# Two heads in one transfer, zero fills on the load queue, a guarded loop, and new weights for a list scheduler

## The chip, the cores and the metric

The kernel runs on one core of a Trainium2 chip. The metric is the device time of one execution in microseconds. TensorE (PE) does the matrix products, VectorE (DVE) and ScalarE (ACT) the elementwise work, GpSimd (POOL) some elementwise work and the indirect transfers, and SyncE (SP) only issues transfers between the chip's memory and the on-chip buffers.

## The reference

Three stages follow each other. Attention has 4 batches, 8 heads, 576 positions and head size 64, and each position sees itself and the 63 before it. Its output, 2304 tokens of 512 numbers, goes through a gated MLP (MoE1, width 2048), and the result through a routed layer (MoE2): a token whose skip score is positive goes to the best of 8 experts (width 1024), the others stay as they are.

```
# attention: scores = q k^T / 8 in a causal window of 64, softmax, times v
h = x @ w_in
sp = np.where(h > 20.0, h, np.log1p(np.exp(np.minimum(h, 20.0))))
x = (h * np.tanh(sp)) @ w_out
...
do_compute = x @ w_skip > 0
logits = x[do_compute] @ w_gate
e_idx = np.argmax(logits, axis=1)
gate_w = softmax(logits)[e_idx]
...
out[do_compute] = x + gate_w * (np.maximum(x @ w1[e], 0.0) @ w2[e])
```

## The kernel before

The 2304 tokens are cut into 6 blocks of 384. For each block there are 4 pairs of heads, 24 pairs in all. For a pair, SP loads q and k (`lqk`) and v (`lv`); S is the scores' matmul, then the softmax on DVE and ACT, PT the transposes of the probabilities, PV the product with v, and xH and xL the two parts of the block's input to MoE1 for that pair's 128 columns (a high part in a rounded format and the rest, so that two or three fast matmuls replace a slow exact one). MoE1 goes over 16 chunks of 128 hidden columns for each block, so 96 chunks: L1 (into `ph`), then mn on DVE, four passes on ACT (u), g on DVE, gH and gL, and L2 (into `po`). The first block's L2 takes the whole weights and is exact; all others take high and low parts. The parts of the weights (cv, ca, w) are also made on DVE and ACT. The first L2 needs all of a chain: PV of pair 3, xH and xL of pair 3, the first chunk's L1, mn, u, g.

The first 8 pairs (`load_nat`, L413) have q and k loaded in the natural layout, in tiles nq and nk that hold four rows and two heads per partition, and transposed on PE (`nat_T`). The others (`load_dvt`) are transposed on DVE. A block that crosses from one batch into the next has two runs of rows, so twice as many transfers. `keep_warm` (L1163) puts dummy matmuls named warm in PE's gaps before the first L2 and at the end of MoE1.

After its MoE1 each block is routed: xs is the evacuated output (`x_evac`, L828), lp or lg the logits, then a chain of small DVE operations (r_mx, r_z, r_oh ...) with a position matmul pp on PE, and the rows are scattered into the table xg_d, by expert. That table must be zero before the first scatter: `fill_zero` sets a tile named nothing to zero on DVE (task fz), `fill_slots` copies it into xg_d (task fs, 17 transfers, on POOL's queue). Every second fill has an fz of its own, and that one waits until the two fills before it have landed. The last block's three tiles go another way to the first experts: xsH and xsL are parts of xs, pick is a 0/1 matrix from the routing, and sel = pick x (xsH + xsL) on PE (24 matmuls for the three tiles) gives the first expert's input at once, which is copied to xgT; E1 is the experts' first matmul (L1221). After all experts, `overflow_round` runs as often as an expert has more tokens than its slots: here not once.

What order the work has is decided when the kernel is built, by a list scheduler (`Plan`, L44). Each task has an engine or a choice of engines with a cost, what it must come after, the buffers it takes, and a due time. The scheduler goes through time, gives each free engine the task that is most urgent, and writes the instructions in that order. Due times are made from T0, D0, D1 and others (first chunk's time and the chunks' distance), shifted by LATE for each kind of task; PRICE, LEAN and SLACK weigh the choice between engines. None of these numbers is known to the chip: each engine runs its instructions in the order written, and waits on semaphores. Transfers on SP take eight semaphores in turn, so that a transfer is issued only when the one eight before it has landed.

Of the kernel before, what the change touches and what calls it, by code (L numbers as in the profile page):

```python
# [22 lines left out]
N1 = 144  # L23


T0, D0, D1, US, UO, WO, LO = 32.22, 5.11, 4.4, 1.64, 5.74, 8, 1.94


LAST = []
GAP, FILL = 0.15, 0.8  # L30
E2B = 0.3
X0 = 2.6
FILL_AT, FILL_BY = 17, 6.0
PRICE3 = dict(P=0, V=0.0, A=0.12, G=0.2, S=0)
AHEAD = 18
EARLY = 8
# [122 lines left out]
TW0 = 38.08
PRICE0 = dict(P=0, V=1.12, A=0.09, G=-0.5, S=0)  # L160
TW = 90.61
PRICE2 = dict(P=0, V=0.99, A=0.94, G=0, S=0)
PRICE = dict(P=0, V=2.15, A=1.08, G=0.63, S=0)
LAT = {("V", "V"): 0.13, ("A", "A"): 0.13, ("A", "V"): 0.14, ("V", "A"): 0.13, ("P", "P"): 0.05}
LATE = dict(wl=-8.1, wa=0.23, wo=0.67, ws=-0.46, wH=-12, lqk=-1.57, nT=-0.3, S=-4.68, ex=4.29, nm=-2.8, PT=-1.37, Pe=4.82, xH=-9.25, L1=0.07, L2=-1.13, me=3.5, n=-5.7, mn=-0.18, ln=2.32, r=-1.08, g=3.72, gH=0.53, xe=7.4, rT=0.57, re=5.95, rl=1.1)
LEAN = {('kT', 'A'): 0.67, ('qT', 'A'): 0.05, ('nm', 'A'): 0.31, ('xH', 'A'): -1.38, ('wo', 'A'): 0.09, ('wH', 'A'): -0.16, ('n', 'A'): -1.26, ('re', 'A'): -0.13, ('xe', 'A'): -0.29, ('nm', 'G'): 1.25, ('wL', 'G'): -0.62, ('gL', 'G'): 1.5}
SLACK = dict(P=0.26, V=0, A=0, G=0.17, S=0.0)


@with_exitstack  # L170
def tile_kernel(
# [24 lines left out]
    XW = DM + 2  # L196
# [4 lines left out]
    xg_d = dram.tile([NE * CAP, XW], F32, name="xg_d")  # L201
# [17 lines left out]
    for p0 in (0, 64):  # L219
        sl = maskA[p0:p0 + 64]  # L220
# [123 lines left out]
    ex = [(e, j) for e in range(NE) for j in range(EW)]  # L344
# [49 lines left out]
    def load_v(pr, dma=SP):  # L394
        blk, hp = divmod(pr, 4)
        vt = rqp.tile([128, 6, 2, D], F32, tag="vt", name="vt", bufs=3)
        vts[pr] = vt
        for g, n, b, s0 in runs(blk):
            z = 2 if s0 == 0 else 0
            if z:  # L400
                G.memset(vt[0:64, 3 * g], 0.0)
            w0 = 3 * g
            if z:
                dma.dma_start(out=vt[64:128, w0], in_=v[b, 2 * hp:2 * hp + 2, 0:64].rearrange("j s d -> s j d"))
                w0 += 1
            lo = s0 + 64 * (w0 - 3 * g) - 64
            nw = 3 * (g + n) - w0
            for j in range(2):
                src = bass.AP(tensor=v.tensor, offset=v[b, 2 * hp + j].offset + D * lo,
                              ap=[[D, 128], [64 * D, nw], [1, D]])  # L410
                dma.dma_start(out=vt[:, w0:w0 + nw, j], in_=src)

    def load_nat(pr):  # L413
        blk, hp = divmod(pr, 4)
        nq = rqp.tile([128, 4, 2, D], F32, tag="rk", name="nq", bufs=4)
        nk = rqp.tile([128, 4, 2, D], F32, tag="rk", name="nk", bufs=4)
        r0 = 0
        for g, n, b, s0 in runs(blk):
            t0 = max(s0 - 64, 0)
            nr = (s0 + 192 * n - t0) // 4  # L420
            for j in range(2):
                SP.dma_start(out=nk[r0:r0 + nr, :, j],
                             in_=k[b, 2 * hp + j, t0:s0 + 192 * n].rearrange("(p r) d -> p r d", r=4))
            for j in range(2):
                SP.dma_start(out=nq[48 * g:48 * (g + n), :, j],
                             in_=q[b, 2 * hp + j, s0:s0 + 192 * n].rearrange("(p r) d -> p r d", r=4))
            r0 += nr
        nat[pr] = (nq, nk, r0)

# [152 lines left out]
    for pr in range(NU // 2):  # L582
        t = unit_time(2 * pr) - 5
        if pr < NPE:
            T(("lqk", pr), one(SS, 2.62 if len(runs(pr // 4)) == 1 else 5.2), lambda e, pr=pr: load_nat(pr), lat=2.3,
              get=[("rk", ("nq", pr)), ("rk", ("nk", pr))], due=t, t0=.7)
            for i in (1, 0):
                T(("nT", pr, i), one(PP, .36), lambda e, pr=pr, i=i: nat_T(pr, i), after=[("lqk", pr)] + ([("S", pr - 1)] if pr else []),
                  get=[(f"po{i}" if pr < 4 else "ps", ("tqk", pr, i))], use=[("nq", pr) if i == 0 else ("nk", pr)])
        else:  # L590
            T(("lqk", pr), one(SS, 3.6 if len(runs(pr // 4)) == 1 else 7.2), lambda e, pr=pr: load_dvt(pr), lat=2.3,
              get=[("rq", ("nq", pr)), ("rk", ("nk", pr))], due=t - 5)
        nd = sum(3 if r[3] == 0 else 2 for r in runs(pr // 4))
        T(("lv", pr), [("S", SP, .53 * nd)], lambda e, pr=pr: load_v(pr, e), lat=2.3,
          get=[("vt", ("vt", pr))], due=unit_time(2 * pr))
    for pr in range(NU // 2):
        if pr < NPE:
# [5 lines left out]
        else:  # L603
# [6 lines left out]
          after=pre + ([("PT", 2 * pr + j - DEEP) for j in range(2)] if early and 2 * pr >= DEEP else []) + ([] if early else [("PT", 2 * pr - 1)]),  # L610
# [89 lines left out]
    for f in range(NF):  # L700
        for kind in ("in", "out"):
# [269 lines left out]
    NS = NE * CAP // 128  # L971
# [6 lines left out]
    def fill_slots(n):  # L978

        if n < NS:  # L980
            G.dma_start(out=xg_d[128 * n:128 * n + 128, :DM].rearrange("p (a c) -> p a c", c=128),
                        in_=nothing[:, :, :128].to_broadcast([128, DM // 128, 128]))
        else:
            G.dma_start(out=xg_d.rearrange("(n p) c -> p n c", p=128)[:, :, DM:XW], in_=nothing[:, :, 128:].to_broadcast([128, NS, 2]))

    for n in range(NS + 1):
        tf = chunk_time(int(FILL_AT)) + FILL_BY * (n // 2)
        if n % 2 == 0:
            T(("fz", n), one(VV, .2), lambda e: fill_zero(), due=tf, t0=tf, after=[("fs", x) for x in range(max(n - 2, 0), n)])
# [442 lines left out]
```

## Time and profile before

| | us |
|---|---|
| time, median of 3 runs | 706.64 (705.81 to 707.05) |
| the profiled execution's time | 707.58 |
| its span in the trace | 705.8 |
| PE busy | 684.6 |
| DVE busy | 444.9 |
| ACT busy | 397.7 |
| POOL busy | 82.0 |

The span goes from the first to the last instruction in the trace; the time has the launch's own edges too. Busy means that the engine worked on data, so the time in which an engine only issues transfers or waits is not in it. [...]

### The profile page before, as it was taken

How to read it: one execution, taken by the hardware profiler on the slowest of the kernel's cores; microseconds unless marked ns; L12 is line 12 of the kernel's file. 1: busy time of each engine (PE TensorE's matmuls, PEld its weight loads, DVE VectorE, ACT ScalarE, POOL GpSimd, SP SyncE). 2: the span in 40 equal slices, each digit the busy share in tenths (PEclk: the TensorE clock that was granted, in tenths of full speed). 3: DMA queues.
4: the chain of work that ended last, by engine and by line, in shares of the span. 5: the costliest groups of instructions: out<-in, count | busy, mean ns of one | idle time of the engine just before them, and what ended most of it. 6: DMA issues, size and time to landing. Idle time of an engine off the chain costs nothing. (4 is left out here: it accounts for less than half of the span.)

```text
span 705.8 us, 13633 instructions
## 1 busy us (share of the span) xinstructions
PE 684.6 (97%) x4921; PEld 583.3 (83%) x4921; DVE 444.9 (63%) x1261; ACT 397.7 (56%) x975; POOL 82.0 (12%) x145
## 2 busy tenths in 40 slices
PE   7999999999999999999999999999999999999993
PEld 7786766788788888888888888888888898998982
DVE  5899999786656556665567655447576553565250
ACT  5778886676666666676556666555652432322220
POOL 3000000212220001000020001012243021111011
PEclk9999999999999999999999999999998999999997
DMA  7889996975523222231221100054472775778000
GB/s 176 210 216 245 283 245 150 207 185 127 110 59 84 41 37 62 46 90 38 39 48 48 51 1 11 19 189 139 133 223 100 253 267 199 270 281 314 1 25 20
DMA packets 141693, 92.54 MB, mean 131 GB/s; under 512 B 110205, under 2 KB 118429, under 8 KB 141616
## 3 DMA queue, kind: packets, MB, share of 16 engines
q1 hardware_dynamic: 137568, 82.90, 42.9%
q0 software_dynamic: 4048, 8.63, 4.1%
q8 instruction: 45, 0.74, 0.4%
q14 instruction: 32, 0.26, 0.1%
HBM read 73.96 MB, written 17.86 MB: 130 GB/s over the span
## 5 line engine op out<-in xcount | busy, mean ns | idle before, releaser
L738 PE MATMUL ph<-xH,w 128*128 128x384 f32 x768 | 222.6, 351 | 1.2 <-DVE g L765 0.5
L789 PE MATMUL po<-w,gH 128*128 128x512 f32 x480 | 152.8, 400 | 0.0
L738 PEld LDWEIGHTS ph<-xH,w 128*128 128x128 f32 x768 | 141.0, 188 | 11.2 <-issue 5.1
L738 PE MATMUL ph<-xL,w 128*128 128x384 f32 x384 | 130.0, 338 | 0.0
L789 PEld LDWEIGHTS po<-w,gH 128*128 128x128 f32 x480 | 88.0, 188 | 14.8 <-DVE gH L317 0.3
L746 ACT ACTIVATE u<-u 128x384 f32<-128x384 f32 x96 | 50.0, 520 | 86.1 <-DVE u L743 82.8
L789 PE MATMUL po<-w,gL 128*128 128x512 f32 x240 | 95.2, 397 | 0.0
L765 DVE SCALAR_TENSOR_TENSOR u<-u,ph 128x384 f32<-128x384 f32 x80 | 44.0, 550 | 70.7 <-ACT u L759 70.0
L738 PEld LDWEIGHTS ph<-xL,w 128*128 128x128 f32 x384 | 72.3, 188 | 2.2 <-issue 1.4
L743 DVE TENSOR_SCALAR u<-ph 128x384 f32<-128x384 f32 x96 | 53.0, 552 | 21.9 <-PE ph L738 21.7
L1221 PEld LDWEIGHTS ph<-xgT,w 128*128 128x128 f32 x512 | 63.7, 190 | 0.9 <-ACT xgT L315 0.3
L532 ACT ACTIVATE P<-P,mx 128x128 f32<-128x128 f32 x144 | 55.8, 389 | 15.4 <-DVE mx L525 15.3
L1221 PE MATMUL ph<-xgT,w 128*128 128x144 f32 x512 | 64.2, 286 | 0.2 <-ACT xgT L315 0.2
L789 PEld LDWEIGHTS po<-w,gL 128*128 128x128 f32 x240 | 45.1, 188 | 12.2 <-DVE gL L774 1.4
L750 ACT ACTIVATE u<-u 128x384 f32<-128x384 f32 x96 | 50.3, 524 | 2.7
L756 ACT ACTIVATE u<-u 128x384 f32<-128x384 f32 x96 | 50.3, 524 | 2.6
L759 ACT ACTIVATE u<-u 128x384 f32<-128x384 f32 x96 | 50.3, 524 | 2.5
L774 DVE TENSOR_TENSOR gL<-u,gH 128x384 fp32r<-128x384 f32 x80 | 46.4, 580 | 5.6 <-ACT gH L315 3.0
L1248 ACT ACTIVATE hH<-ph 128x288 fp32r<-128x288 f32 x32 | 13.1, 409 | 62.1 <-PE ph L1221 43.3
L789 PE MATMUL po<-w,g 128*128 128x512 f32 x96 | 44.4, 598 | 0.0
L1265 PE MATMUL po<-w,hH 128*128 128x512 f32 x128 | 42.6, 414 | 0.0
L277 POOL DMA_INDIRECT xg_d<-xs,r_si x18 | 18.3, 1019 | 158.2 <-DVE u L765 76.9
(159 smaller groups left out, 1014.2 us busy)
## 6 DMA issues: line engine op xcount, KB each, us to landing
st<-in_moe_w_dram SPq DMA_DIRECT2D x64, 256.0 KB
w<-in_moe_w_dram SPq DMA_DIRECT2D x32, 512.0 KB
w<-in_moe_w_in_dram SPq DMA_DIRECT2D x16, 512.0 KB
w<-in_moe_w_out_dram SPq DMA_DIRECT2D x16, 512.0 KB
out_dram<-xs SPq DMA_DIRECT2D x18, 256.0 KB
xg<-xg_d SPq DMA_DIRECT2D x16, 257.0 KB
ca<-w SPq DMA_DIRECT2D x16, 256.0 KB
xg_d<-nothing POOLq DMA_DIRECT2D x16, 256.0 KB
```

What stands on the lines that cost most here:

```text
L532: A.activation(P[:, i], P[:, i], AF.Exp, bias=mx[:, 0, u % 2, i:i + 1], scale=-1.0, accum_out=mx[:, 1, u % 2, i:i + 1])
L738: PE.matmul(phs[c], a[:, kk], b[:, kk], start=kk == 0 and n == 0, stop=kk == NK - 1 and n == len(terms) - 1)
L743: V.tensor_scalar(u, phs[c], 20.0, None, op0=ALU.min)
L746: A.activation(us[c], us[c], AF.Exp)
L750: A.activation(us[c], us[c], AF.Square, bias=1.0)
L756: A.activation(us[c], us[c], AF.Ln, scale=0.5, bias=half_t[c])
L759: A.activation(us[c], us[c], AF.Exp, scale=-1.0)
L765: V.scalar_tensor_tensor(o, us[c], 1.0, phs[c], op0=ALU.subtract, op1=ALU.mult)
L774: eng.tensor_tensor(gL, us[c], gH.bitcast(F32), op=ALU.subtract)
L789: PE.matmul(po[m, t], a[:, ts], b, start=f == 0 and n == 0, stop=f == NF - 1 and n == len(terms) - 1)
L1221: PE.matmul(ph[:, i], w1_t[e, kk][:, 128 * f:128 * f + 128], xgT[e][:, kk, :N1], start=kk == 0, stop=kk == NK - 1)
L1265: PE.matmul(po2[e, s], a[:, f, ss], b, start=f == 0 and n == 0, stop=f == 7 and n == 2)
```

## The change

One. `load_nat` takes both heads of a pair in one transfer for k and one for q, where there were two each. The pieces stay 256 bytes long, as the two heads lie apart in memory: 48 transfers for the first 8 pairs become 24. Two. The 17 fills of xg_d are issued by SP in place of POOL, with other costs in the plan, and are due from chunk 21 on in place of 17. Three. The scheduler's numbers are new throughout. Four. The overflow loop stands in a condition.

```diff
-T0, D0, D1, US, UO, WO, LO = 32.22, 5.11, 4.4, 1.64, 5.74, 8, 1.94
+T0, D0, D1, US, UO, WO, LO = 20.57, 3.54, 4.21, 1.68, 5.52, 2.09, 3.4
...
-FILL_AT, FILL_BY = 17, 6.0
+FILL_AT, FILL_BY = 21, 6.0
...
-PRICE = dict(P=0, V=2.15, A=1.08, G=0.63, S=0)
+PRICE = dict(P=0, V=2.33, A=1.47, G=0.63, S=0)
...
-            for j in range(2):
-                SP.dma_start(out=nk[r0:r0 + nr, :, j],
-                             in_=k[b, 2 * hp + j, t0:s0 + 192 * n].rearrange("(p r) d -> p r d", r=4))
-            for j in range(2):
-                SP.dma_start(out=nq[48 * g:48 * (g + n), :, j],
-                             in_=q[b, 2 * hp + j, s0:s0 + 192 * n].rearrange("(p r) d -> p r d", r=4))
+            hs = slice(2 * hp, 2 * hp + 2)
+            SP.dma_start(out=nk[r0:r0 + nr], in_=k[b, hs, t0:s0 + 192 * n].rearrange("j (p r) d -> p r j d", r=4))
+            SP.dma_start(out=nq[48 * g:48 * (g + n)], in_=q[b, hs, s0:s0 + 192 * n].rearrange("j (p r) d -> p r j d", r=4))
...
-            G.dma_start(out=xg_d[128 * n:128 * n + 128, :DM].rearrange("p (a c) -> p a c", c=128),
-                        in_=nothing[:, :, :128].to_broadcast([128, DM // 128, 128]))
+            SP.dma_start(out=xg_d[128 * n:128 * n + 128, :DM].rearrange("p (a c) -> p a c", c=128),
+                         in_=nothing[:, :, :128].to_broadcast([128, DM // 128, 128]))
...
-        T(("fs", n), one(GG, 1.04), lambda e, n=n: fill_slots(n), after=[("fz", n - n % 2)], lat=5, due=tf + 2)
+        T(("fs", n), one(SS, 1.9 if n < NS else 1.0), lambda e, n=n: fill_slots(n), after=[("fz", n - n % 2)], lat=5, due=tf + 2)
...
-    with tc.For_i(0, nr, 1):
-        overflow_round()
+    with tc.If(nr > 0):
+        with tc.For_i(0, nr, 1):
+            overflow_round()
```

The order of instructions, at three places. The first is SP's queue from the start of pair 0's loads (nk and nq) to v of pair 2 (vt_636 before, vt_517 after). A row with x2 is two transfers. Before, rows from pair 1 on (pair 0 has the same two rows as pair 1):

```order
L422 DMA nk_170<-in_k_dram 96x4x64 x2
L425 DMA nq_169<-in_q_dram 96x4x64 x2
L644 DMA w2_245<-in_moe_w_in_dram 128x4x256
L422 DMA nk_284<-in_k_dram 96x4x64 x2
L425 DMA nq_283<-in_q_dram 96x4x64 x2
L404 DMA vt_343<-in_v_dram 64x2x64
L411 DMA vt_343<-in_v_dram 128x5x64 x2
L422 DMA nk_360<-in_k_dram 96x4x64 x2
L425 DMA nq_359<-in_q_dram 96x4x64 x2
```

After, from pair 1 on as well:

```order
L422 DMA nk_166<-in_k_dram 96x8x64
L423 DMA nq_165<-in_q_dram 96x8x64
L404 DMA vt_174<-in_v_dram 64x2x64
L411 DMA vt_174<-in_v_dram 128x5x64 x2
L422 DMA nk_249<-in_k_dram 96x8x64
L423 DMA nq_248<-in_q_dram 96x8x64
L641 DMA w2_288<-in_moe_w_in_dram 128x4x256
L422 DMA nk_308<-in_k_dram 96x8x64
L423 DMA nq_307<-in_q_dram 96x8x64
```

Each pair of transfers has become one, pair 0's v moved ahead of pair 2's q and k, and the second weight chunk behind them. Counted through, v of pair 2 is transfers 35 to 37 before and 23 to 25 after.

The second place is DVE at the end of MoE1, where the last block's third tile (xs_6597 before, xs_6562 after) is split and the first tile's routing begins with r_mx. Before:

```order
L317 CAST xsH_6566<-xs_6576 128x512
L1085 TENSOR_TENSOR xsL_6567<-xs_6576,xsH_6566 128x512
L317 CAST w29_6595<-st_6515 128x512
L317 CAST w31_6600<-st_6551 128x512
L317 CAST xsH_6566<-xs_6597 128x512
L1085 TENSOR_TENSOR xsL_6567<-xs_6597,xsH_6566 128x512
L899 TENSOR_REDUCE r_mx_6624<-lp_6602 128x1
```

After:

```order
L830 TENSOR_SCALAR xs_6533<-po_5836 128x512
L317 CAST xsH_6523<-xs_6533 128x512
L317 CAST w29_6546<-st_6475 128x512
L341 TENSOR_TENSOR w29_6546<-st_6475,w29_6546 128x512
L830 TENSOR_SCALAR xs_6562<-po_5840 128x512
L317 CAST xsH_6523<-xs_6562 128x512
L896 TENSOR_REDUCE r_mx_6577<-lp_6555 128x1
```

The xsL are gone from DVE (POOL has them), and the evacuations of xs, which ACT did, stand here. Further on, the picks of the three tiles stood in one row before (`L1094 TENSOR_SCALAR pick<-iota_122,row_all 128x256 x3`) behind all three tiles' routing; after, each stands behind its own tile's, and on PE eight selects stand before the third tile's pp, eight behind it and eight after a last few warm matmuls.

The third place is SP in the middle of MoE1, where the fills (xg_d from nothing) now stand among the back copies of weights (ca) and the attention loads of later blocks. After:

```order
L978 DMA xg_d_58<-nothing_156 128x4x128 x2
L679 DMA ca_1794<-w5_907 128x512
L411 DMA vt_1818<-in_v_dram 128x6x64 x2
L978 DMA xg_d_58<-nothing_156 128x4x128 x2
L679 DMA ca_1891<-w7_1056 128x512
L476 DMA rq_1909<-in_q_dram 32x12x32
```

Before, they were POOL's:

```order
L476 MEMSET rk_1920 128x64
L981 DMA xg_d_58<-nothing_156 128x4x128 x4
L835 COPY xs_2063<-tok_98 128x1
L835 COPY xs_2066<-tok_98 128x1
L835 COPY xs_2069<-tok_98 128x1
L981 DMA xg_d_58<-nothing_156 128x4x128 x2
```

A fill now stands behind the transfers ahead of it in SP's queue, and the transfers after it behind the fill's wait for fz.

## Rows read from the trace of the kernel before

**Rows 1.** The page's first part: busy time of each engine.

```profile
PE 684.6 (97%) x4921; PEld 583.3 (83%) x4921; DVE 444.9 (63%) x1261; ACT 397.7 (56%) x975; POOL 82.0 (12%) x145
```

**Rows 2.** Windows: busy us (instructions) by engine, PE clock, DMA share, GB/s.

```profile
10.00:46.00 36.00, 32.65 (x488) 28.59 (x480) 30.85 (x116) 29.00 (x97) 1.76 (x11) 0.95 0.83 207
20.00:22.50 2.50, 2.44 (x28) 2.01 (x26) 2.46 (x11) 2.50 (x8) 0.20 (x1) 1.00 0.28 62
...
46.00:120.00 74.00, 73.39 (x445) 51.18 (x446) 72.49 (x177) 58.68 (x138) 0.51 (x3) 1.00 0.91 231
120.00:200.00 80.00, 78.09 (x525) 63.82 (x524) 57.68 (x191) 52.84 (x137) 18.75 (x28) 1.00 0.69 150
...
538.00:547.00 9.00, 8.19 (x71) 8.08 (x70) 4.58 (x49) 0.96 (x4) 3.10 (x3) 0.62 0.09 34
...
694.40:705.80 11.40, 0.02 (x1) 0.00 (x0) 0.75 (x1) 0.00 (x0) 0.98 (x1) 0.68 0.03 8
```

**Rows 3.** SP: timeline to 30 us, then lines L422 and L411.

```profile
24.35 0.64 SPq L404 DMA_DIRECT2D vt<-in_v_dram  x1
...
L422 SPq DMA_DIRECT2D nk<-in_k_dram x24: 534/602/938, 1.3 to 80.9; - x24
...
L411 SPq DMA_DIRECT2D vt<-in_v_dram x64: 368/532/1953, 10.7 to 385.8; - x64
```

**Rows 4.** Timeline of PE to 52 us (idle before, releaser).

```profile
9.63 0.89 PE L509 MATMUL sc<-kT,qT 64*64 64x128 f32 x24 [1.55 <-ACT qT L315]
...
31.83 0.57 PE L564 MATMUL pv<-PT,vt 128*64 128x64 f32 x12 [0.32 <-DMA vt<-in_v_dram]
...
48.26 2.74 PE L789 MATMUL po<-w,g 128*128 128x512 f32 x6
```

**Rows 5.** Timeline of DVE, 27 to 50 us.

```profile
39.72 0.55 DVE L580 TENSOR_TENSOR xL<-pv,xH 128x384 fp32r<-128x384 f32 x1
...
45.45 0.54 DVE L765 SCALAR_TENSOR_TENSOR g<-u,ph 128x384 f32<-128x384 f32 x1
```

**Rows 6.** Timelines of DVE, POOL and PE around 540 us.

```profile
534.98 1.39 DVE L317 CAST xsH<-xs 128x512 fp32r<-128x512 f32 x1
536.40 1.64 DVE L1085 TENSOR_TENSOR xsL<-xs,xsH 128x512 fp32r<-128x512 f32 x1
537.96 0.15 DVE L899 TENSOR_REDUCE r_mx<-lp 128x1 f32<-128x8 f32 x1
...
542.32 0.87 DVE L1094 TENSOR_SCALAR pick<-iota,row_all 128x256 fp32r<-128x256 int16 x3
...
534.70 2.79 POOL L341 TENSOR_TENSOR w<-st,w 128x512 fp32r<-128x512 f32 x2 [6.03 <-DVE w L317]
...
535.82 1.91 PE L874 MATMUL lp<-wgs,xf 128*128 128x9 f32 x16
...
547.32 2.96 PE L1221 MATMUL ph<-xgT,w 128*128 128x144 f32 x22 [0.20 <-ACT xgT L315]
```

**Rows 7.** Lines L1400 and L1427 in the last 11 us.

```profile
L1400 POOLq EVENT_SEMAPHORE  x4: 17/43/1807, 696.0 to 698.0; - x4
...
L1400 POOLq INC_SWDGE_SEM  x1: 727/727/727, 698.1 to 698.1; - x1
...
L1400 POOLq EVENT_SEMAPHORE  x12: 42/43/43, 701.5 to 702.5; - x12
...
L1400 POOLq COMPARE_BRANCH  x2: 38/40/41, 698.8 to 702.5; - x2
...
L1427 POOLq DRAIN  x3: 45/103/2282, 702.7 to 705.5; - x3
```

**Rows 8.** The fills: tile nothing, and SP's waits for PE.

```profile
L981 POOL DMA_DIRECT2D xg_d<-nothing x16: 750/752/982, 124.2 to 184.0; - x16
...
  DMA xg_d<-nothing: 3.2, 3
...
SPq L411 <- PE pv L564: 46.4, 8, 10.2
```

More of the change, by code (lines that the diff above doesn't have):

```diff
@@ L156, in emit @@
             self.tasks[k]["fn"](e[1])
[L159 to L162, printed above, removed]
-PRICE = dict(P=0, V=2.15, A=1.08, G=0.63, S=0)
+TW0 = 30.94
+PRICE0 = dict(P=0.0, V=2.28, A=0.5, G=-0.5, S=0.0)
+TW = 309.39
+PRICE2 = dict(P=0.0, V=1.26, A=2.91, G=0.0, S=0.0)
+PRICE = dict(P=0.0, V=2.33, A=1.47, G=0.63, S=0.0)
 LAT = {("V", "V"): 0.13, ("A", "A"): 0.13, ("A", "V"): 0.14, ("V", "A"): 0.13, ("P", "P"): 0.05}
-LATE = dict(wl=-8.1, wa=0.23, wo=0.67, ws=-0.46, wH=-12, lqk=-1.57, nT=-0.3, S=-4.68, ex=4.29, nm=-2.8, PT=-1.37, Pe=4.82, xH=-9.25, L1=0.07, L2=-1.13, me=3.5, n=-5.7, mn=-0.18, ln=2.32, r=-1.08, g=3.72, gH=0.53, xe=7.4, rT=0.57, re=5.95, rl=1.1)
-LEAN = {('kT', 'A'): 0.67, ('qT', 'A'): 0.05, ('nm', 'A'): 0.31, ('xH', 'A'): -1.38, ('wo', 'A'): 0.09, ('wH', 'A'): -0.16, ('n', 'A'): -1.26, ('re', 'A'): -0.13, ('xe', 'A'): -0.29, ('nm', 'G'): 1.25, ('wL', 'G'): -0.62, ('gL', 'G'): 1.5}
-SLACK = dict(P=0.26, V=0, A=0, G=0.17, S=0.0)
+LATE = dict(wl=-9.64, wa=-0.1, wo=-3.47, ws=-4.07, wH=-11.22, lqk=-4.23, nT=-11.43, S=-14.23, ex=-0.53, nm=-4.0, PT=0.94, Pe=7.68, xH=-13.18, L1=2.57, L2=0.89, me=1.15, n=-4.49, mn=-0.61, ln=-5.67, r=-7.61, g=3.04, gH=3.02, xe=2.94, rT=1.62, re=-6.31, rl=2.98, rs=-1.25, lg=13.87, ro=-1.68, eH=16.04, rc=1.8, PV=-0.21, wL=2.42, ga=-3.86, sL=-1.97, xo=13.29, eL=4.54, m2=6.01, bl=18.08, wb=-0.93, ke=-20.26, m1=16.67, se2=-11.46, sl=7.64, el=-0.26, qT=2.69, fz=-9.43, bt=-20.62, se=-13.56, sH=11.09, sd=-1.3, wg=-1.88, tg=9.05, fs=-2.81, xgH=-0.09, sm=9.36, oh=-8.74, su=7.71, xL=-4.21, we=3.45, pl=-8.44, gL=2.75, pi=-2.04, co=-1.2, pm=-0.37, dm=8.62, kT=-2.92, fi=-2.37, mx=3.12, L2t=14.66, ep=-14.67, rq=0.13, lv=-0.43)
+LEAN = {('kT', 'A'): 0.38, ('qT', 'A'): -1.31, ('nm', 'A'): 0.39, ('xH', 'A'): -1.88, ('wo', 'A'): -0.82, ('wH', 'A'): -0.15, ('n', 'A'): -1.04, ('re', 'A'): -1.33, ('xe', 'A'): 0.36, ('nm', 'G'): 0.37, ('wL', 'G'): -2.59, ('gL', 'G'): 1.14}
+SLACK = dict(P=0.04, V=0.0, A=0.0, G=0.17, S=0.0)
 @with_exitstack
@@ L584, in tile_kernel @@
         if pr < NPE:
-            T(("lqk", pr), one(SS, 2.62 if len(runs(pr // 4)) == 1 else 5.2), lambda e, pr=pr: load_nat(pr), lat=2.3,
+            T(("lqk", pr), one(SS, 1.8 if len(runs(pr // 4)) == 1 else 2.3), lambda e, pr=pr: load_nat(pr), lat=2.3,
               get=[("rk", ("nq", pr)), ("rk", ("nk", pr))], due=t, t0=.7)
@@ L593, in tile_kernel @@
         nd = sum(3 if r[3] == 0 else 2 for r in runs(pr // 4))
-        T(("lv", pr), [("S", SP, .53 * nd)], lambda e, pr=pr: load_v(pr, e), lat=2.3,
+        T(("lv", pr), [("S", SP, max(1.6, .5 * nd))], lambda e, pr=pr: load_v(pr, e), lat=2.3,
           get=[("vt", ("vt", pr))], due=unit_time(2 * pr))
@@ L980, in fill_slots @@
         if n < NS:
-            G.dma_start(out=xg_d[128 * n:128 * n + 128, :DM].rearrange("p (a c) -> p a c", c=128),
-                        in_=nothing[:, :, :128].to_broadcast([128, DM // 128, 128]))
+            SP.dma_start(out=xg_d[128 * n:128 * n + 128, :DM].rearrange("p (a c) -> p a c", c=128),
+                         in_=nothing[:, :, :128].to_broadcast([128, DM // 128, 128]))
         else:
-            G.dma_start(out=xg_d.rearrange("(n p) c -> p n c", p=128)[:, :, DM:XW], in_=nothing[:, :, 128:].to_broadcast([128, NS, 2]))
+            SP.dma_start(out=xg_d.rearrange("(n p) c -> p n c", p=128)[:, :, DM:XW], in_=nothing[:, :, 128:].to_broadcast([128, NS, 2]))
     for n in range(NS + 1):
-        tf = chunk_time(int(FILL_AT)) + FILL_BY * (n // 2)
+        tf = chunk_time(FILL_AT) + FILL_BY * (n // 2)
         if n % 2 == 0:
             T(("fz", n), one(VV, .2), lambda e: fill_zero(), due=tf, t0=tf, after=[("fs", x) for x in range(max(n - 2, 0), n)])
-        T(("fs", n), one(GG, 1.04), lambda e, n=n: fill_slots(n), after=[("fz", n - n % 2)], lat=5, due=tf + 2)
+        T(("fs", n), one(SS, 1.9 if n < NS else 1.0), lambda e, n=n: fill_slots(n), after=[("fz", n - n % 2)], lat=5, due=tf + 2)
     T(("wg",), one(SS, 1.0), lambda e: load_wgs(), due=chunk_time(2), lat=3)
```

## The prediction

> **What bounds the kernel now.** I read the page's totals first [rows 1]: PE is busy for 684.6 of 705.8 us (97%), DVE for 444.9. A share over the whole span doesn't say where the other 21 us are, so I took windows next [rows 2]. From 46 us on PE is as good as full: 73.39 of 74 us, 78.09 of 80, then stretches without a gap up to 694.4 us. DVE is nearly full as well up to 120 us (72.49 of 74), but has some 22 us of 80 free between 120 and 200. So the end follows from four things: the moment when PE starts to be dense (the first L2), a fixed amount of PE work, the holes in it, and what comes after the last matmul. Two stretches have holes. Between 0 and 46 us much of what PE does is warm, dummy matmuls that fill gaps. And in 538 to 547 us PE runs at a granted clock of 0.62 as a mean; that is where MoE1 hands over to the experts. After 694.4 us PE does nothing for 11.4 us.
>
> The change does not touch PE's real work: it issues the same transposes, S, PV, L1, L2 and expert matmuls. Only the warm ones go from 275 to 238, and they stand in gaps. So I cost three places, start, handover and tail, and ask whether the middle stays full.
>
> **Start.** SP issues the loads one after the other, at 602 ns each for the keys' 96- to 48-partition transfers and 532 ns for vt [rows 3]. An issue hardly depends on how much it moves: most vt transfers have 384 to 768 pieces of 256 bytes, those of nk 192 to 384, and the vt ones cost less. So I price a merged transfer (768 pieces) like the one it replaces, 0.6 us; the other end is twice as much, which would leave nothing. The vt load of pair 2 is the 35th to 37th transfer in SP's old order and the 23rd to 25th in the new one, since 24 of q and k become 12. That is 12 x 0.6 = 7.2 us less issuing ahead of it; it went out at 24.35 us [rows 3], and PE still waited for it at 31.83 us [rows 4]. That it was the issuing that held this back shows in 20 to 22.5 us: SP issues without a pause, and the DMA engines are only 0.28 busy, against 0.83 over 10 to 46 us [rows 2].
>
> [...]
>
> How much of the 7.2 us reaches PE? Not all, since DVE comes next. From 10 to 46 us DVE is busy 30.85 of 36 us [rows 2], so 5.15 us idle. The first S, at 9.63 us [rows 4], can come two issues earlier (1.2 us), as pair 0 has four transfers and will have two. If all of DVE's idling went, L2(0) would start 5.15 + 1.2 = 6.4 us earlier: the upper bound. The lower bound is 0. Inside these I follow the chain that ends in L2(0): PV of pair 3, xL(3) at 39.72, mn and four ACT passes, g at 45.45 [rows 5], L2(0) at 48.26 [rows 4]. In the new order S of pair 2 stands ahead of more warm matmuls, the vt wait is gone, and DVE has the same softmax and weight work before xL(3), with some lqs and xs work traded with ACT. With the durations of the old rows xL(3) then comes at about 36, and the rest of the chain is unchanged. I take **-3.5 us** (0 to -6.4), a little over half of the upper bound.
>
> **Handover.** At the end of MoE1 the last block's three tiles are routed, and PE can begin the experts only when all 24 selects are done. In the old order DVE does xsH and xsL of tile 2 at 534.98 and 536.40, and only then the first step of the routing, r_mx, at 537.96 [rows 6]. These two took 1.39 and 1.64 us, while POOL ran two operations of its own from 534.70 [rows 6]. Then all three tiles go through the routing before the three picks, at 542.32, and E1 starts at 547.32 [rows 6]. The new order gives the three xsL to POOL, so r_mx may start some 2 us earlier; and each tile's pick now follows its own routing, so eight selects run while the next tile is still being routed. The price: xs is evacuated on DVE rather than ACT (three operations of about 0.6 us), and xsL on POOL takes about 1.4 us by the POOL row, which ends before tile 2's selects. Against a full 2 us stands that pp, the position matmul, still follows rl of all three tiles on PE, which ends near 537.7 [rows 6]. Most of what is saved is the serial part: selects of two tiles under the routing. I take **-2.0 us** (0 to -3.4: the 9 us of the window 538 to 547 at 0.62 of the clock [rows 2] hold work that at 1.00 would take 5.6).
>
> **Tail.** The condition around the overflow loop changes what each engine runs after its last work, as the loop's count is zero. Now POOL's INC_SWDGE_SEM ends at 698.8 us (698.1 and 0.727), but its 12 waits of the loop's exit run only from 701.5 to 702.5 [rows 7]. So 2.7 us lie between a branch and its target on POOL, then 1.0 us of waits, then a DRAIN of 2.28 us from 702.7 [rows 7] that the end follows. In the changed program the not-taken path goes right to the end, the branch stands ahead of the wait for the last output's landing, which ended at about 698.0 (the longest wait, 1.807 us [rows 7]), and POOL has no twelve waits there. So the 2.7 us should lie under that wait, at least its 1.8 to 2.1 us, and 1.0 us falls away: -2.8 to -3.2 us, less some tenths for the extra branch. I take **-2.7 us** (+0.8, if the branch is merely added with its own 0.7 us of a second INC, to -3.2).
>
> **Middle.** Seventeen fills of 256 KB move from POOL's queue to SP's. On POOL they cost 0.75 us each [rows 8] and no engine waited; on SP some 0.5 us each by the rows of SP's other transfers [rows 3], 8.5 us over 70 us in which SP is free most of the time. But fz, the memset on DVE, waits for the fills two before it. It did wait, 3.2 us in three times [rows 8], while PE lost 1.9 of the 80 us from 120 to 200 for all reasons together, and DVE had 22 of them free [rows 2]: that free time covers such a wait. On SP a fill stands behind loads that wait for PE: vt loads waited 46.4 us in 8 times, the longest 10.2 [rows 8]. Such a wait would now also hold a fill, then fz, then DVE's queue: the next mn, g and gH. I take **0** (-1.5, if most of those 1.9 us go, to +3, two waits of DVE that outlast what its lead covers). The remaining weights move work between DVE, ACT and POOL while PE is full, and cost or give nothing as long as it stays full.
>
> **Sum.** -3.5 - 2.0 - 2.7 = -8.2 us. The profiled execution took 707.58 us, 1.8 more than its span, and is 0.94 above the median of the runs, 706.64. So 699.4 for an execution like the profiled one, and **698.4** against the median. The best ends together give -6.4 - 3.4 - 3.2 - 1.5 = -14.5, that is 692.1.
>
> **Rivals.** A change of 0.2% (1.4 us) is about what a measurement of this kernel can tell from none.
>
> *The start is bound by something else* (0.20). The DMA engines are 0.83 busy over 10 to 46 us; if q and k in 256-byte pieces fill them, or if ACT's chain holds DVE, L2(0) moves by only about 0.5 us, and the time is 706.64 - 0.5 - 2.0 - 2.7 = 701.4. For it speaks ACT's 29.00 of 36 us busy [rows 2]; against it the 0.28.
>
> *The tail stays* (0.13). POOL's branch across the loop's body is still there in the changed program. If its 2.7 us come after the last INC again, or if the drain that ends the program is tied to that INC and not to the waits, the tail gives nothing: 706.64 - 5.5 = 701.1. The rows speak for a cost of the branch; that it can hide under a wait no row shows. [...]
>
> *The fills stall DVE* (0.07), the case on the slow side. Its place is fz in 120 to 200 us, behind fills that are behind vt and rq loads on SP. To end slower than before it has to take back 8.2 us and 1.4 more: two of the eight waits of 5 us each, PE standing for all of it, which is inside the longest 10.2 us of [rows 8] but far from the 1.8 us that DVE waits now. It gives 708 or more.
>
> *Nothing reaches the end* (0.07): the start as in the first rival, the tail as in the second, and a DVE wait of some 2 us: within 1.4 us of 706.64.
>
> *More than forecast* (0.08): DVE becomes full from the first S on, and handover and tail reach their bounds: 692 to 694.
>
> **How the numbers follow.** The forecast, all three gains with their spread, holds 0.45, from 694.5 to 700.5. Faster is the sum of all cases but two, 0.86; within 0.2% 0.07; slower 0.07. The range goes from 692.5, just above the sum of the best ends, to 705.0, which leaves out the two bad cases and a little of the best.
>
> **What would show it.** L2(0) at about 45 us in place of 48.26, with no PE wait for vt, and the DMA share in 15 to 25 us clearly above 0.28. E1 starts some 5.5 us earlier than 547.32 (3.5 from the start, 2 of its own), with r_mx before 536 less the shift, and less PE time at the lower clock. From the last matmul to the end about 8.7 us in place of 11.4. PE losing no more than 2 us between 120 and 200 us. I am wrong if L2(0) does not move, if POOL still sits for 2.7 us after its INC, or if DVE shows waits for fills of several us with PE holes behind them.

## The result and the profile after

The changed kernel took 695.92 us (median of 4 runs, 694.94 to 696.17) against 706.31 for the kernel before, measured beside it (705.81 to 707.05): a ratio of 0.984 [0.982, 0.986]. It is faster, by somewhat more than was forecast (698.4), and inside the range. But all four terms of the sum, the middle's 0 among them, were wrong in size. The page of the new kernel begins:

```profile
PE 678.2 (98%) x4884; PEld 582.5 (84%) x4884; DVE 450.6 (65%) x1268; ACT 392.2 (57%) x963; POOL 74.2 (11%) x133
```

Read beside [rows 1], PE has lost 6.4 us of busy time. Part of that is dummy matmuls, so shares don't say where the span's 12.25 us went. (The medians are 10.4 us apart; the traces show 1.9 more, mostly since the profiled execution of before, 707.58 us, was itself 1.3 above the median.) Its windows, cut like [rows 2] but with the handover and the tail where they now lie (the clock is a share of PE's full speed; the DMA share counts the time that packets took, so it can pass 1):

```profile
10.00:46.00 36.00, 31.05 (x458) 27.50 (x457) 31.14 (x117) 30.45 (x99) 1.77 (x11) 0.95 1.10 255
20.00:22.50 2.50, 2.50 (x47) 2.10 (x40) 1.80 (x15) 1.62 (x10) 0.30 (x2) 0.59 0.85 212
46.00:120.00 74.00, 73.88 (x455) 52.65 (x455) 72.63 (x191) 62.02 (x153) 1.56 (x7) 1.00 0.95 223
120.00:200.00 80.00, 80.00 (x581) 66.74 (x580) 59.12 (x189) 56.34 (x146) 4.12 (x9) 1.00 0.66 143
531.00:540.00 9.00, 8.71 (x65) 8.44 (x64) 6.30 (x48) 0.63 (x4) 4.01 (x4) 0.64 0.13 48
687.20:693.57 6.37, 0.01 (x1) 0.00 (x0) 0.75 (x1) 0.00 (x0) 0.98 (x1) 0.80 0.03 8
```

PE is now full from 120 to 200 us (80.00 of 80, from 78.09), the DMA engines are busy where SP's issuing had left them idle (0.85 in place of 0.28 over 20 to 22.5 us), and the tail is 6.4 us, from 11.4. The clearest reading is when PE reaches the same piece of work in either trace. L2(n) is a mark in the row of L2's matmuls on PE's timeline, the same one in every trace: L2(0) is the first of them, L2(2) the 7th, L2(11) the 34th, L2(17) the 58th, L2(20) the 85th and L2(32) the 193rd. The numbers in brackets, in the expectations too, are not chunks beyond the first: they count three records to a chunk in the first block, where the trace has six. L2(11) lies in chunk 5, L2(20) begins chunk 14, and L2(32) lies in chunk 26, so the stretch between the last two holds the end of the first block and most of the second.

| landmark | before, us | after, us | gained so far | gained in this stretch | forecast |
|---|---|---|---|---|---|
| L2(0) | 48.26 | 48.72 | -0.46 | -0.46 | 3.5 |
| L2(20) | 126.70 | 124.91 | 1.79 | 2.25 | 0 |
| L2(32) | 194.46 | 189.42 | 5.04 | 3.25 | 0 |
| end of the last L2 | 534.26 | 527.47 | 6.79 | 1.75 | 0 |
| E1 | 547.32 | 539.99 | 7.33 | 0.54 | 2.0 |
| end of matmuls | 694.42 | 687.21 | 7.21 | -0.12 | 0 |
| end of the span | 705.81 | 693.57 | 12.25 | 5.04 | 2.7 |

Before L2(0) the changed kernel has also done eight transposes of keys and queries that the old one does later, so the first line flatters the old one, and the second the new one, by some 0.7 us (eight such transposes take PE 0.65 to 0.75 us in the old trace). So the start gave next to nothing, the handover half a microsecond, the tail twice its term, and more than half of the gain came from the middle, which I had put at 0.

**The start.** What answers to [rows 3] on SP's timeline:

```profile
20.42 0.65 SPq L404 DMA_DIRECT2D vt<-in_v_dram  x1
21.11 1.16 SPq L411 DMA_DIRECT2D vt<-in_v_dram  x2
```

v of pair 2 is issued 3.9 us earlier (7.2 us of issuing were counted), and the wait for vt is gone. PE's timeline, what answers to [rows 4], and one row of DVE's:

```profile
8.98 0.89 PE L506 MATMUL sc<-kT,qT 64*64 64x128 f32 x24 [0.43 <-ACT qT L315]
17.61 0.99 PE L550 MATMUL tp<-ident,P 128*128 128x128 f32 x6 [2.74 <-DVE P L545]
...
48.72 1.48 PE L786 MATMUL po<-w,g 128*128 128x512 f32 x3
```

```profile
16.57 0.43 DVE L650 TENSOR_SCALAR cv<-w 128x512 int32<-128x512 int32 x1 [2.48 <-DMA w<-in_moe_w_in_dram]
```

In place of the old wait there is another, further ahead: DVE stands 2.48 us for the second chunk of w_in, with pair 0's normalisation (P, L545) queued behind it, and PE stands 2.74 us for that P. Behind that wait PE's granted clock is at its lower level (0.50) from 18.6 to 22.0 us (0.59 in the window from 20 to 22.5 us, 1.00 before).

**The handover.** DVE, then POOL, then PE, for [rows 6]:

```profile
527.50 1.64 DVE L341 TENSOR_TENSOR w<-st,w 128x512 fp32r<-128x512 f32 x1
529.07 0.68 DVE L830 TENSOR_SCALAR xs<-po 128x512 f32<-128x512 f32 x1
529.78 0.92 DVE L317 CAST xsH<-xs 128x512 fp32r<-128x512 f32 x1
530.62 0.15 DVE L896 TENSOR_REDUCE r_mx<-lp 128x1 f32<-128x8 f32 x1
...
531.08 0.99 DVE L913 SCALAR_TENSOR_TENSOR first<-r_z,r_d 128x8 f32<-128x8 f32 x1
...
530.77 1.27 POOL L1082 TENSOR_TENSOR xsL<-xs,xsH 128x512 fp32r<-128x512 f32 x1 [0.36 <-DVE r_mx L896]
...
529.80 0.66 PE L841 MATMUL rtp<-ident,xs 128*128 128x128 f32 x4 [1.04 <-DVE xs L830]
530.29 3.11 PE L871 MATMUL lp<-wgs,xf 128*128 128x9 f32 x16
533.26 0.17 PE L926 MATMUL pp<-cum,ones 128*128 128x8 bf16 x1
539.99 1.23 PE L1218 MATMUL ph<-xgT,w 128*128 128x144 f32 x7 [0.29 <-DVE xgT L317]
```

From the end of the last L2 to the first pp it takes 5.8 us (4.1 before), since the last tile's evacuation xs stands on DVE behind a weight part of 1.64 us and PE waits 1.04 us for it. Then the 16 lp take 3.11 us, where they took 1.91 in [rows 6]: the granted clock is 0.55 over them, and was 1.00. From the first pp to E1 it takes 6.7 us (8.95 before). The routing did overlap with the selects; the way into it got longer by almost as much.

**The tail.** POOL's sequencer at the guard, L1397, and at the end, L1425, for [rows 7]:

```profile
L1397 POOLq EVENT_SEMAPHORE  x4: 17/43/1759, 689.1 to 689.3; - x4
L1397 POOLq COMPARE_BRANCH  x1: 45/45/45, 688.6 to 688.6; - x1
L1397 POOLq INC_SWDGE_SEM  x1: 444/444/444, 691.1 to 691.1; - x1
...
L1425 POOLq DRAIN  x3: 40/107/1128, 691.6 to 693.3; - x3
```

The twelve waits are gone, and so is the gap of 2.7 us behind the branch: 0.5 us lie between compare and first wait. What I had not forecast: INC takes 0.44 us in place of 0.73, and the DRAIN 1.13 in place of 2.28.

### The profile page after: what moved, and what is told of

Its sections match the earlier page's. It is cut to its first block, busy times and chain, and to the rows that moved or that the text cites. A ratio compares the mean times of both kernels' runs of the same rounds, so it can differ in the third digit from the quotient of the medians.

```text
span 693.6 us, 13440 instructions
## 1 busy us (share of the span) xinstructions
PE 678.2 (98%) x4884; PEld 582.5 (84%) x4884; DVE 450.6 (65%) x1268; ACT 392.2 (57%) x963; POOL 74.2 (11%) x133
## 5 line engine op out<-in xcount | busy, mean ns | idle before, releaser
L786 PE MATMUL po<-w,gH 128*128 128x512 f32 x480 | 154.4, 403 | 0.0
L341 DVE TENSOR_TENSOR w<-st,w 128x512 fp32r<-128x512 f32 x48 | 34.3, 732 | 0.7
```

Of the source, the lines that this page charges most:

```text
L786: PE.matmul(po[m, t], a[:, ts], b, start=f == 0 and n == 0, stop=f == NF - 1 and n == len(terms) - 1)
```

## The experiments

Runs made together share a chip, and each ratio is to the kernel before on that chip, where it took 711 to 712 us; on the chip of the result it took 706. The changed kernel itself has a ratio of 0.978 there (run a_again).

### One part at a time, in the old order

**Merged transfers alone (b_merge).** The old kernel and its order of tasks, with the two new lines of `load_nat`:

```diff
-            for j in range(2):
-                SP.dma_start(out=nk[r0:r0 + nr, :, j], ...)
...
+            hs = slice(2 * hp, 2 * hp + 2)
+            SP.dma_start(out=nk[r0:r0 + nr], in_=k[b, hs, t0:s0 + 192 * n].rearrange("j (p r) d -> p r j d", r=4))
...
```

> The kernel before with q and k of both heads in one transfer, and not one instruction in another place. Theory D (the DMA engines, not SP's issuing, bound the first 15 us): the first pair's q and k land no earlier, the DMA share of 0 to 10 us rises from 0.72 towards 1.0 at the same GB/s, the second L2 chunk start moves by under 1.5 us and the time by 0 to -1.5 us. Rival I (issuing bounds it, as predicted): 12 issues of 0.6 us less ahead of v of pair 2, L2(0) 3.5 us earlier, the time near 702.8.

Measured: 707.63 us, ratio 0.995 [0.993, 0.997]. PE's timeline:

```profile
29.39 0.92 PE L561 MATMUL pv<-PT,vt 128*64 128x64 f32 x24
...
45.62 1.88 PE L786 MATMUL po<-w,g 128*128 128x512 f32 x4
```

L2(0) comes 2.6 us earlier than in [rows 4], without a wait for vt, and L2(11) 2.9 us earlier. So the start's term was about right for the merging by itself, though v of pair 2 is issued only 1.9 us earlier (22.49 us) and part of the gain may be the clock's: the granted clock is 1.00 over 10 to 46 us, where before, with a stretch at the lower level just behind the waits for vt, it was 0.95. Of the 2.9 us, 2.5 are lost again between L2(20) and L2(32), which take 70.3 us.

**The condition alone (b_if).**

```diff
-    with tc.For_i(0, nr, 1):
-        overflow_round()
+    with tc.If(nr > 0):
+        with tc.For_i(0, nr, 1):
+            overflow_round()
```

> The kernel before with the condition around the overflow loop alone. Theory T (the tail changes by the condition, and by more than was predicted): from the last matmul to the end of the span 6.4 us in place of 11.4, the time 5 us shorter, about 701.3. As predicted: 2.7 shorter, 703.6. Rival (the branch costs as before, the tail of the changed kernel is short for another reason): no change, 706.3.

Measured: 708.0 us, 0.995 [0.993, 0.997]; from the last matmul to the end 8.59 us, that is 2.8 less than before. POOL's sequencer:

```profile
L1400 POOLq EVENT_SEMAPHORE  x4: 17/43/43, 702.2 to 702.4; - x4
L1400 POOLq COMPARE_BRANCH  x1: 53/53/53, 699.2 to 699.2; - x1
L1400 POOLq INC_SWDGE_SEM  x1: 740/740/740, 702.5 to 702.5; - x1
...
L1428 POOLq DRAIN  x3: 45/107/2280, 703.3 to 706.1; - x3
```

The 3.0 us behind the branch are still there, but now they lie over the wait for the last landing, of which nothing is left (43 ns where it was 1.8 us). That is the mechanism and the size of the forecast. INC and DRAIN are unchanged. What POOL does in the 3.0 us no run shows. Against the rival, they need not lengthen the program: the tail is 8.59 us in place of 11.4.

**The fills on SP's queue, alone (b_fillq).** In the old order, `G.dma_start` becomes `SP.dma_start` in `fill_slots`.

> The kernel before with the 17 fills on SP's queue in place of POOL's, all other instructions in their old places. Theory F (the second block's holes on PE came from DVE waiting for fills): DVE's 3.2 us of waits for fills go, and so do the 1.3 us at 189 us and the shorter holes, 3 us less, about 703.3. Rival W (they came from the order that the old numbers gave): DVE's waits may go, PE's holes stay, within 0.7 us of 706.3. Rival S (SP holds the fills back): DVE waits longer, 1 to 3 us slower.

Measured: 709.23 us, 0.997 [0.996, 0.999]. Two things happen that work against each other. The middle gets worse: L2(20) to L2(32) takes 73.8 us, against 70.3 in b_merge and 71.8 in b_if, which were taken beside it, and PE stands once for 3.7 us behind DVE:

```profile
150.53 0.69 PE L738 MATMUL ph<-xH,w 128*128 128x384 f32 x1 [3.67 <-DVE u L765]
```

The tail becomes shorter, 7.68 us in place of 11.4, with the loop and its waits unguarded:

```profile
L1400 POOLq EVENT_SEMAPHORE  x16: 17/43/1732, 701.4 to 705.3; - x16
L1400 POOLq INC_SWDGE_SEM  x1: 436/436/436, 703.4 to 703.4; - x1
...
L1427 POOLq DRAIN  x3: 40/103/1131, 705.5 to 707.2; - x3
```

INC and DRAIN are shorter just as in the changed kernel, and 0.4 us lie behind the branch. So the second half of the tail's gain belongs to the fills.

**The new numbers alone (b_weights).** The old kernel with the new tables of T0, LATE, LEAN and the rest, from which the scheduler makes an order by the old costs of the transfers:

```diff
-T0, D0, D1, US, UO, WO, LO = 32.22, 5.11, 4.4, 1.64, 5.74, 8, 1.94
+T0, D0, D1, US, UO, WO, LO = 20.57, 3.54, 4.21, 1.68, 5.52, 2.09, 3.4
...
```

> The kernel before with the new numbers of the scheduler alone (two transfers for each of q and k, fills on POOL, no condition). Theory W: the new order takes the holes out of the second and third block: from chunk 17 to chunk 32 of L2 89 us in place of 93.4, as in the changed kernel; start and tail as before; the time 5 to 6.5 us shorter, about 700.5. Rival F (the fills' move did that): 93 us there, and the time within 2 us of 706.3.

Measured: 716.06 us, 1.007 [1.004, 1.009], slower. L2(20) to L2(32) takes 76.3 us. So the numbers are not what made this stretch better; here they help only together with the transfers that they were made for. Behind it they do help by themselves: from L2(32) to the end of the last L2, b_weights takes 338.0 us as the changed kernel does, and before 339.8. That is the 1.75 us of the table.

**No fill's memset waits (b_fz).** In the old order, every `fz` after the first sets another tile, which no transfer reads, so that DVE never waits for a fill:

```diff
-        V.memset(nothing[:, :, :129], 0.0)
+        z = idle if n else nothing
+        w = 95 if n else 129
+        V.memset(z[:, :, :w], 0.0)
...
```

> The kernel before, with the repeated memsets (all but the first) on a tile that no transfer reads, so that DVE waits for no fill; fills on POOL as before. Theory F (PE's holes in the second block come from DVE standing for fills): DVE's waits for fills are 0, L2(20) to L2(32), 67.8 us in the trace of before and 70.3 to 71.8 in the two experiments on another chip, falls to 65 to 66, as in the changed kernel (64.5), and the time by 2 to 5 us. Rival O (they come from the old order of DVE's other work): it stays above 67, and the time within 1.5 us.

Measured: 720.34 us, 1.012 [1.009, 1.016]: slower, where I had looked for a gain. The rows of POOL, DVE and PE:

```profile
124.75 3.26 POOL L984 DMA_DIRECT2D xg_d<-nothing  x4 [13.43 <-DVE mx L536]
...
141.71 0.43 DVE L317 CAST w<-ca 128x512 fp32r<-128x512 f32 x1 [8.57 <-DMA ca<-w]
...
149.69 0.79 PE L789 MATMUL po<-w,gH 128*128 128x512 f32 x1 [11.24 <-ACT xs L831]
```

The memset's wait had spaced the fills: before, eight pairs of them start 7 to 10 us apart. Without it nine go out within 8.5 us; the copies of weights coming back (ca) are late, DVE stands 8.57 us and ACT up to 13.5 us for them, and PE then stands 11.24 us behind ACT. The wait that I had taken for a small cost was a throttle.

### One part undone, in the new order

**The changed kernel again (a_again)**, unchanged, to have it on the chip of the next three.

> The changed kernel again, on the chip of the three that go with it. Expected as measured: 0.984 of the time before, a tail of 6.4 us, L2(0) at 48.7 us. If this chip, as the one of the first four experiments, has the old order's later fills land later, the ratio is lower (0.978 to 0.984), since the changed kernel's memsets waited for no fill.

Measured: 696.49 us, 0.978 [0.975, 0.981]; L2(0) at 48.95, L2(20) to L2(32) 64.51, tail 6.3.

**Fills back on POOL's queue (a_pool)**, in the new order, `SP.dma_start` back to `G.dma_start` in `fill_slots`.

> The changed kernel with the 17 fills back on POOL's queue, nothing else moved. Theory Q (the fills' queue sets part of the tail: POOL's last increment and drain are longer after more transfers of its own): tail 8.6 us in place of 6.4, and the second block unchanged, so 2.2 us slower than the changed kernel. Rival B (the queue also makes the holes of the second block): tail 8.6, and L2(17) to L2(32) 92 us or more in place of 89.2, 5 us slower. Rival N (neither): as the changed kernel.

Measured: 698.27 us, 0.980 [0.977, 0.983]. L2(20) to L2(32) is 64.52, as with the fills on SP. The tail is 8.71 us, with an INC of 0.74 us and a DRAIN of 2.28. So in the new order the queue that carries the fills is worth 2.4 us, all of it in the tail.

**Without the condition (a_noif)**: the two lines of b_if, the other way round.

> The changed kernel without the condition around the loop. Theory G (with the fills off POOL's queue the 2.7 us gap on POOL is gone anyway, so the condition saves only the exit's twelve waits): tail 7.7 us as with the fills on SP alone, 1.3 us slower than the changed kernel. Rival P (the condition is what hides the gap, as predicted): the gap is back, tail 9 us or more, 2.7 us slower.

Measured: 697.72 us, 0.981 [0.977, 0.984]; tail 7.67 us, INC 0.435, DRAIN 1.131. Beside tails of 6.3 to 6.6 in the executions of the changed kernel and its variants below (7.1 in a_split), the condition is worth 0.6 to 1.4 us here, at most half of the 2.8 alone, since without the gap behind the branch there is only the time of the twelve waits to save.

**Merging undone (a_split)**: the old lines of `load_nat` in the new order.

> The changed kernel with the merging alone undone: two transfers for each of q and k, all else in its place. Theory M (the merging is worth the same in the new order as it was alone in the old): L2(2) 2.9 us later than 54.5, 3 us slower than the changed kernel. Rival (in the new order the wait for a weight chunk and the DMA engines set the start, so issuing isn't the bound): L2(2) within 1 us, no slower than 1 us.

Measured: 703.93 us, 0.990 [0.987, 0.993]. L2(0) comes at 51.23 and L2(11) at 82.89, 2.5 and 4.7 us later than in the changed kernel. SP issues pair 2's v at 24.54 us again, and PE stands for late keys after the first L2 too:

```profile
24.54 0.65 SPq L404 DMA_DIRECT2D vt<-in_v_dram  x1
...
68.86 0.57 PE L438 MATMUL tqk<-ident,nk 112*128 112x112 f32 x4 [1.67 <-DMA nk<-in_k_dram]
...
87.47 0.57 PE L438 MATMUL tqk<-ident,nk 112*128 112x112 f32 x4 [1.01 <-DMA nk<-in_k_dram]
```

So the merging works in the new order too, and is worth more there: 6.8 us by L2(20), against 2.9 in the old order at the same place.

### Two waits of the new order, and both together

**The second weight chunk earlier (a_w2).** In `Plan.emit`, that load is taken ahead of pair 0's v:

```diff
...
+            at = {s[2]: i for i, s in enumerate(steps)}
+            w = steps.pop(at["wl", ("in", 1)])
+            steps.insert(at["lv", 0], w)
...
```

> The changed kernel with one transfer moved: the second chunk of w_in is issued before v of pair 0 rather than behind q and k of pair 2. Theory D (DVE stands 2.5 us at 14 us for this chunk with pair 0's normalisation behind it, and the DMA engines are full there): that wait falls under 0.5 us, PT of pair 0 comes 2 us earlier, L2(0) 1.5 to 2.5 us earlier, and the time 1.5 to 2.5 us below the changed kernel. Rival L (the loads that are pushed back take its place): L2(0) within 0.5 us, no change.

Measured: 695.98 us, 0.977 [0.974, 0.980], no different from a_again. DVE's wait for the weight is gone, but keys take its place, and L2(0) stands at 48.82:

```profile
14.92 0.52 PE L440 MATMUL tqk<-ident,nk 96*128 96x96 f32 x4 [1.78 <-DMA nk<-in_k_dram]
```

**The last evacuation on ACT (a_xe).**

```diff
+            if k == ("xe", 5, 2):
+                e = ("A", self.tasks[k]["engines"][0][1], e[2])
```

> The changed kernel with the evacuation of the last tile (xs of tile 2) on ACT, in the same place of the order. Theory H (this evacuation waits on DVE behind a weight cast and a weight part of 1.64 us, and PE waits 1.0 us for it): PE's wait for xs goes, from the last L2 to E1 11.3 us in place of 12.5, the time 1.2 us shorter. Rival A (ACT has its own cast and xf ahead, or the routing of tile 0 is what counts): 0 to -0.3 us.

Measured: 695.63 us, 0.977 [0.974, 0.980], not to be told from a_again. PE's wait for xs is gone; then it waits for r_oh:

```profile
533.20 0.17 PE L931 MATMUL pp<-r_oh,triu 128*128 128x8 bf16 x1 [0.77 <-DVE r_oh L923]
```

Last L2 to E1 is 11.9 us. In the executions that leave this part of the changed kernel alone it is 11.5 to 12.9, so this run alone settles little. How long PE's granted clock is at its lower level there accounts for most of the spread: 3.4 us in a_split and a_w2 (11.6 and 11.5 us), 6.8 in the other four (12.5 to 12.9). It is 6.8 us in a_xe too, and beside those four a_xe is shorter by 0.6 us or more.

**Both, with two more moves (a_best):** the second chunk early, pair 0's transposes of P ahead of pair 2's of q and k, the last evacuation on ACT, and one weight part (L341) behind the picks.

> The changed kernel with moves at both ends: the second chunk of w_in before v of pair 0 on SP, PT of pair 0 ahead of pair 2's transposes on PE (those waited 1.8 us for their load in the run before), the evacuation of the last tile on ACT, and one weight part of 1.64 us on DVE moved from before the last routing to behind the second pick. Theory: PT of pair 0 at about 15 us in place of 17.6, L2(0) 1.5 to 2 us earlier; from the last L2 to E1 11 us in place of 12.5; together 2.5 to 3.5 us below the changed kernel, ratio to before 0.973. Rival (DVE has its work packed from 20 us on, whatever comes before): L2(0) within 0.5 us of 48.7, the end gains 1 us.

Measured: 693.95 us, 0.977 [0.973, 0.981]. L2(0) comes 0.96 us earlier, which is inside the spread of the executions with the changed kernel's own start (47.5 to 50.1), and by L2(11) nothing of it is left (+0.28). The handover is 10.2 us, 1.3 below the shortest of the others, with 3.4 us at the lower clock as in those. The span is 691.7 us, 1.9 less than the changed kernel's; the ratio's interval holds that of a_again, so it is likely, but not shown, that a_best is faster than the change.

## Why the prediction was right, and where not

**The start (-3.5, measured +0.5).** By the prediction's own sign ("I am wrong if L2(0) does not move") this part failed. One trace could mislead, as L2(0) goes with the granted clock: in the executions with the new start it is 47.53 us where the clock is 1.00 over 10 to 46 us (a_pool), 48.72 and 48.95 at 0.95, and 49.60 and 50.05 at 0.91 (a_noif, a_xe). But the four with the old start, all at 0.95, have 47.95 to 49.06, so the finding stands. The step on the issuing was right in kind: merged, the load is issued earlier (by 3.9 us, where 7.2 were counted), the DMA share in the stretch rises above 0.28, the vt wait goes, and by itself it brings 2.6 to 2.9 us (b_merge). For one transfer issuing is the smaller part: in the changed kernel the merged ones of k take 0.63 us to issue and 6.2 from issue to landing (medians of 12). But SP issues in a row, and the same bytes in half as many transfers gave those 2.9 us. The step that failed is the next one, "In the new order S of pair 2 stands ahead of more warm matmuls, the vt wait is gone, and DVE has the same softmax and weight work before xL(3)". I took the new order as neutral at the start. It isn't: with the transfers merged in both, it reaches L2(0) 3.1 us and L2(11) 2.6 us later than the old order (b_merge). With the transfers split it reaches L2(11) at 82.89 us (a_split), while the old order does so at 77.9 to 79.0 in the four executions that keep the old start. So the new order costs some 3 to 4 us there, the merging gives 3 to 5, and what I forecast as a gain in time was used up. That is the first rival's sign, an L2(0) that moves by no more than 0.5 us, with a cause that I had not named. a_w2 and a_best show that the waits in it stand behind one another: with the weight's gone, the keys' comes. Over 10 to 46 us the DMA engines are now at a share of 1.10, and in a_w2 the transfer brought forward put another back.

**The middle (0, measured -7.25 from the start of the first L2 to the end of the last).** "I take 0 (-1.5, if most of those 1.9 us go ...)" was the worst step. I had read how long PE is idle, and L2(20) to L2(32) also has time in which PE is recorded as busy: the windows cut at these two matmuls, first of before, then of after, hold the same number of matmuls.

```profile
126.70:194.46 67.76, 65.85 (x466) 53.77 (x466) 48.52 (x161) 43.90 (x112) 13.80 (x23) 1.00 0.74 156
```

```profile
124.91:189.42 64.51, 64.51 (x466) 53.95 (x466) 47.48 (x153) 46.23 (x118) 0.68 (x4) 1.00 0.66 150
```

Of the 3.25 us, 1.9 was idle and 1.3 was in matmuls that took longer. What these depend on is seen across the runs. The second column is how long DVE and ACT together stood for ca, the copies of weights, over 108 to 192 us:

| kernel | waits for ca, us | L2(20) to L2(32), us |
|---|---|---|
| after | 1.7 | 64.51 |
| a_pool | 3.3 | 64.52 |
| a_split | 4.1 | 64.52 |
| a_again | 4.7 | 64.51 |
| before | 12.6 | 67.76 |
| b_if | 14.9 | 71.78 |
| b_merge | 15.8 | 70.30 |
| b_fillq | 18.3 | 73.81 |
| b_weights | 21.3 | 76.34 |
| b_fz | 31.9 | 80.29 |

In the new order this stretch is the same to 0.01 us in all eight traces, with the fills on either queue and q and k merged or not: PE is full and sets the time. In the old order, and in b_weights, it is not: it waits for copies whose landing differs from run to run. b_if has the old order's program up to the tail, and lost 4 us more here than the profiled execution. That is likely why the kernel before takes 706 us on one chip and 711 on others, and the changed kernel does not, but no trace of before was taken on those, so it stays an inference. That late copies of weights cost time here is shown by b_fz (later copies, more time). That the new order gains by their lead rests on the table alone, and which of the new numbers gives it was not taken apart. From L2(32) on the new numbers give 1.75 us whatever the transfers, as b_weights shows. The rival in which fills stall DVE is not what b_fillq shows: DVE's waits for fills are 4.6 us there over 108 to 192 us, no longer than in b_if and b_merge (6.8 and 5.8, fills on POOL), while the waits for ca grew, and the stretch took 2.0 to 3.5 us more than in those two. In the changed kernel DVE waits for no fill.

**The handover (-2.0, measured -0.5).** Both mechanisms are seen in the rows: 2.2 us gained from pp to E1, 1.7 lost ahead of it. The term that was mis-sized is the price "xs is evacuated on DVE rather than ACT (three operations of about 0.6 us)": the operation itself takes 0.68, but it stands behind a weight part of 1.64 us, and behind PE's wait for it the granted clock was low (0.55) while the lp ran, which the price did not have either. Besides, the place varies more than the change moves it. With the old handover it took 11.8 to 13.1 us in five traces, with the new one 11.5 to 12.9 in six, means of 12.55 and 12.29. Of these, the executions with 6.8 us at the lower clock took 12.8 to 13.1 in the old order and 12.5 to 12.9 in the new one, those with 3.4 us 11.8 and 12.2, and 11.5 and 11.6: the change is worth 0.3 to 0.4 us either way.

**The tail (-2.7, measured -5.0).** For the condition the mechanism and the size were right, -2.8 alone. The step that failed is that the fills' move was priced only in the middle. All traces make a square of the times from the last matmul to the end, in us:

| | loop bare | loop guarded |
|---|---|---|
| fills on POOL's queue | 11.4 to 11.8 | 8.6 and 8.7 |
| fills on SP's queue | 7.7 and 7.7 | 6.3 to 7.1 |

Against the 11.4 of before, the fills' move is worth 3.7 us by itself, the condition 2.8, and both together 5.0: what either saves of the gap behind the branch counts once. The rival in which the tail stays is ruled out by b_if.

**The sum.** -8.2 us were forecast, and the two traces differ by 12.25: 0.46 lost at the start, 7.25 gained in the middle, 0.54 at the handover and 5.04 in the tail, with 0.12 lost among the experts. The forecast time came out within 2.5 us of the result because start and handover, forecast at 5.5 together, gave almost nothing, while the middle and the tail gave 9.6 more than their terms. That the errors partly cancel is luck. The range held, but its middle was made of the wrong parts; of the runs' medians on the other chips, where the old kernel is slower by 5 us, it could say nothing.

## What to carry to other kernels

Where an order of instructions and the transfers that it waits for are changed together, the parts are not a sum: the new numbers, the merged loads and the moved fills each had another worth, or another sign, in the other order. A stretch in which the bound engine looks 97% busy can still hold 5% of time (3.25 of 67.76 us here), and it shows when the same work is timed between two of its instructions in both traces. And a wait that looks like a small loss may be what spaces transfers (without it, b_fz took 1.012 of the time before): before removing it, ask what it holds back.

## What the hardware showed that I had not expected

- Seventeen transfers issued from POOL's queue some 500 us ahead of the end still cost time at the end: INC_SWDGE_SEM takes 0.73 to 0.74 us and the longest of POOL's closing DRAINs 2.28 with them (before, b_if, a_pool), 0.44 and 1.13 without (after, b_fillq, a_noif). The indirect transfers stay on POOL in all of them.
- The gap of 2.7 to 3.0 us behind POOL's branch over the loop's body occurs only when the fills are POOL's (before, b_if, a_pool); without them 0.4 to 0.5 us lie there (after, b_fillq, a_noif). What lies in the gap, no run here shows.
- Merging two transfers of 256-byte pieces made the DMA engines busier in the first 10 us, but hardly made the bytes come faster there: their share goes from 0.72 at 180 GB/s (before) to 0.92 at 192 (b_merge), and PE starts on pair 0's q at 7.10 us, behind a wait of 0.40 for it, where it started at 6.95.
- A DVE operation on 128x8 numbers that takes 0.15 to 0.17 us took 0.99 us beside POOL's xsL (`first` at 531.08), and in a_best 0.77 beside a weight part on POOL and 0.99 beside xsL; each ends within 0.03 us of the POOL operation. That this is one reason why xsL on POOL brought less than its time on DVE is likely, as `first` lies on the routing's chain, but was not tested.
